# Converting float64 gate weights beside the expert items alone, in two buffers, with one multiplication handed to ScalarE and GpSimd

## The chip, the cores and the metric

The kernel runs on one core of a Trainium2 chip. The core has a matrix engine (TensorE, PE in the profile, with its weight loads shown apart as PEld), a vector engine (VectorE, DVE), ScalarE (ACT), GpSimd (POOL) and SyncE (SP), which issues the transfers. They run side by side and wait for each other by semaphores. Each engine takes its instructions strictly in the order of its own queue. The metric is the device time of one execution in microseconds (us), as the median of several runs.

## The reference, cut to what matters

```python
def _moe_ref(x, domain_probs, w1, w2):          # x: 1536 tokens x 512, out of a windowed attention
    p = domain_probs / (domain_probs.sum(-1, keepdims=True) + 1e-09)
    out = np.zeros((N, D), dtype=np.float32)
    for e in range(E):                           # 4 experts, d_ff 1024
        h = np.maximum(x @ w1[e], 0.0)
        out += p[:, e:e + 1] * (h @ w2[e])
    return out

def _moe2_ref(x, w_a, w_b, w_out):               # d_ff 1536
    a = x @ w_a
    b = x @ w_b
    return a * b @ w_out

attn_out = _attn_ref(q, k, v, n_sink, window)    # 2 batches, 8 heads, 768 positions, 64 wide
x = attn_out.transpose(0, 2, 1, 3).reshape(B * S, H * D)
x = _moe_ref(x, ...)
return _moe2_ref(x, moe2_w_a, moe2_w_b, moe2_w_out)
```

The three weights of the last, gated layer (`w_a`, `w_b`, `w_out`) arrive as float64. [...]

## The kernel before

**Precision.** All products are made from float32 numbers cut into a high and a low part (`split`: the high part is a rounded copy, the low part the difference). A product is then three matmuls: high by high, high by low, low by high (`three`).

**Stages.** The program is recorded in three pieces, and each is put in order and issued by `nc.run()`. The first has the attention of batch 0 and the first two pieces of the experts for batch 0. The second has the attention of batch 1 beside most of the experts' pieces for batch 0. The third, in the trace from about 375 us on, has no attention. It has the last expert piece of batch 0, then 16 *items* of experts for batch 1 (about 395 to 645 us; below the expert items), then 12 items of the gated layer for batch 0 (from about 645 us on), then 12 for batch 1 (to the end).

**One item.** `seven` makes the up products of an item by a Strassen-like scheme of seven products in two banks of PSUM, `m` and `n`. Between them intermediate results have to leave the banks: copies `r1`, `r5`, `u2` (in the trace `r` and `u`, by ScalarE or VectorE) and sums `c0` to `c2` (`c`, by VectorE). Only then may TensorE write the bank again. Six output tiles of the item before are laid between these products (`dh`, `dl`, `hh`, `hl` in the trace).

**Weights of an item.** `ups` loads `rawu` (one buffer), forms four sums of its quarters (`sums`) and splits seven blocks into `uh` and `ul` (two buffers each). For batch 1 of the experts and of the gated layer the split blocks come back from memory (`store`, `keeping`), so the 16 expert items of batch 1 have no splitting to do, and the 12 gated items of batch 0 have all of it. While the gated items of batch 0 run, the expert results of batch 1 are also transposed into tokens (`turned`: three transposes of `y` into a bank, a copy `x` out of it, then sums and splits).

**Converting the gate weights** (`gate_weights`). There are 36 parts of 128x512 numbers: for each of 12 blocks one of `w_a`, one of `w_b`, one of `w_out`. A part is loaded into one of two buffers `raw64` (in the trace `raw`; low words `l`, high words `h`, interleaved). Two halves `t` and `u` of a buffer `tu`, of which there is one, take the steps: ScalarE squares the high word (`tf`), VectorE makes five instructions on them, and a last addition goes to VectorE or GpSimd. Then the part is written to memory (`gu` or `gd`), from where `ups` and `downs` load it as `rawu` and `rawd`. How fast the parts are recorded beside the items is set by `PARTS` and `PARTS_LATE`: 1.6 parts an item to the end of the expert items, then 1.2.

**What sets the order.** `Plan.run` is a list scheduler. Each instruction has a cost and a due time; at each step the engine that can begin first takes its most urgent ready instruction. An instruction with two ways (`either`, used by `copied` for ScalarE or VectorE, and by `combined` for GpSimd or VectorE) goes to whichever takes it first. `shares` marks the instructions that the planner takes to need a port that VectorE and GpSimd have in common: every GpSimd instruction but a memset, and VectorE's with SBUF operands alone, either two of them or a copy or scalar operation. `begin` puts off such a one until the other engine's has ended. Nothing of these times reaches the chip: only the order and the choice of engine do, with the waits that the data need.

Of the kernel before, what the change touches and what calls it, by code (L numbers as in the profile page):

```python
# [9 lines left out]
F32 = mybir.dt.float32  # L10
F32R = mybir.dt.float32r
BF16 = mybir.dt.bfloat16
I32 = mybir.dt.int32
U32 = mybir.dt.uint32
ACTF = mybir.ActivationFunctionType
ALU = mybir.AluOpType
# [3 lines left out]
P = 128  # L20
# [75 lines left out]
class Plan:  # L96
# [163 lines left out]
    def run(self, ahead=8, idle=None):  # L260
# [15 lines left out]
        ready = {e: [] for e in "TVSGD"}  # L276
# [31 lines left out]
        for _ in nodes:  # L308
            best = None
            for e, some in ready.items():  # L310
                if e == "T":
                    some = [x for x in some if rank[x["n"]] < first + ahead]
                if not some:
                    continue
                now = max(free[e], min(x["ready"] for x in some))
                if e not in "TD":
                    while True:
                        can = [x for x in some if x["ready"] <= now and fits(x, e, now)]
                        if can:
                            break  # L320
                        later_ = [x["ready"] for x in some if x["ready"] > now]
                        if not later_:
                            break
                        now = min(later_)
                    if not can:
                        continue
                    x = min(can, key=urgent)

                    soon = [
                        y for y in some if now < y["ready"] < now + x["ways"][e][0]  # L330
                        and y["due"] < min(x["due"] - self.MORE, at + self.NEAR) and fits(y, e, y["ready"])
                    ]
                    if soon:
                        y = min(soon, key=urgent)
                        short = [z for z in can if now + z["ways"][e][0] <= y["ready"]]
                        x = min(short, key=urgent) if short else y
                        now = max(now, x["ready"])

                    start = begin(x, e, now)
                    if start > now:  # L340
                        short = [
                            z for z in can if begin(z, e, now) == now and now + z["ways"][e][0] < start + self.NEAR_PORT
                        ]
                        x, start = (min(short, key=urgent), now) if short else (x, start)
                    now = start
                else:
                    x = min((x for x in some if x["ready"] <= now), key=urgent)
                if best is None or now < best[0]:
                    best = now, x, e
            now, x, e = best  # L350
            for f in x["ways"]:
                ready[f].remove(x)
            x["e"], (cost, x["calls"], shared) = e, x["ways"][e]
            x["cost"] = cost
            if e == "T" and idle:
                if any(self.region(args[0] if args else kw["out"])[0] == idle[0].tensor.name for _, args, kw in x["calls"]):
                    idle = None
                elif not free[e]:
                    x["idle"] = self.IDLE_FIRST, idle
                elif now - free[e] > self.IDLE:  # L360
                    x["idle"] = int((now - free[e] - self.IDLE_LEFT) / self.IDLE_COST), idle
            free[e] = now + cost
            if shared:
                port[e] = now + cost
            order.append(x)
            if e == "T":
                at = max(at, x["at"])
                done.add(rank[x["n"]])
                while first in done:
                    first += 1  # L370
            for u in users[x["n"]]:
                y = nodes[u]
                y["ready"] = max(y["ready"], now + cost + lag(x, y))
                left[u] -= 1
                if not left[u]:
                    release(y)
# [12 lines left out]
def tile_kernel(ctx, tc, a0, a1, vs, limit, dp, w1, w2, wa, wb, wo, out):  # L389
# [11 lines left out]
    NV = E * FP  # L401
# [906 lines left out]


    CONVERT_STEPS = 11  # L1310
    PARTS, PARTS_LATE = 1.6, 1.2

    def gate_weights(room):

# [18 lines left out]
        for n, (_, dst) in enumerate(parts):  # L1333
            raw, ahead = ahead, fetch(n + 1) if n + 1 < len(parts) else None
            for _ in range(3):
                yield
            tu = room("tu")
            l, h, t, u = raw[:, :, 0], raw[:, :, 1], tu[:, 0:512], tu[:, 512:1024]
            tf, uf = t.bitcast(F32), u.bitcast(F32)
            nc.scalar.activation(out=tf, in_=h.bitcast(F32), func=ACTF.Square)  # L1340
            nc.vector.tensor_scalar(
                out=u, in0=h, scalar1=3, scalar2=0x3FFFFFFF, op0=ALU.logical_shift_left, op1=ALU.bitwise_and
            )
            yield
            nc.vector.scalar_tensor_tensor(
                out=u, in0=h, scalar=-0x40000000, in1=u, op0=ALU.bitwise_and, op1=ALU.bitwise_or
            )
            yield
            nc.vector.scalar_tensor_tensor(
                out=uf, in0=tf, scalar=W_LOW * W_LOW, in1=uf, op0=ALU.is_ge, op1=ALU.mult  # L1350
            )
            yield
            nc.vector.tensor_scalar(out=t, in0=u, scalar1=-0x800000, scalar2=None, op0=ALU.bitwise_and)
            yield
            nc.vector.scalar_tensor_tensor(
                out=tf, in0=l.bitcast(U32), scalar=2.0 ** -52, in1=tf, op0=ALU.mult, op1=ALU.mult
            )
            yield
            combined(uf, uf, tf, add)
            yield  # L1360
            yield
            nc.sync.dma_start(out=dst, in_=form(uf, dst))
            yield

    def convert_steps(parts):

        return CONVERT_STEPS * parts
# [94 lines left out]
    with ExitStack() as st:  # L1462
# [103 lines left out]
        with ExitStack() as s2:  # L1566
# [10 lines left out]

            plains[-1].bank, plains[-1].apart = bank, True
            plain = Expert(items[own - 1], x, wu, wd, y0, bank)
            room = lambda name: p.g.tile([P, 1024], I32, tag=name, name=name, bufs={"raw64": 2, "tu": 1}[name])  # L1580
            w = Stream(gate_weights(room))
            for n, _ in enumerate(run([plain], bank, plains[-1], freed)):
                u.to(UP_STEPS * (own + (n + 1) / ITEM_STEPS))
                d.to(DOWN_STEPS * (own - 1 + (n + 1) / ITEM_STEPS))
                w.to(convert_steps(PARTS * (n + 1) / ITEM_STEPS))
            flagged = Stream(need_general(bank))
            open_ = {}
            run_ = [Expert(it, x, wu, wd, y1, bank, True, open_) for it in items[own:own + NV]]
# [13 lines left out]
            for n, _ in enumerate(run(run_, bank, plain, freed)):  # L1602
# [10 lines left out]
                for b, i in enumerate((3, NV + 2)):  # L1613
                    k = n - start(i) - 10
                    if k > 0:
                        tr[b].to(k / ITEM_STEPS)
                at, turn = 1 + (n + 1) / ITEM_STEPS, NV + 1
                w.to(convert_steps(PARTS * min(at, turn) + PARTS_LATE * max(at - turn, 0)))
            d.finish()
            rest_of(run_[-1])  # L1620
            nc.run()
# [62 lines left out]
```

## Time and profile before

| | |
|---|---|
| median of 3 runs | 938.14 us (936.51 to 940.12) |
| the profiled execution | 936.52 us, of which its span, first to last instruction, 934.6 us |
| busy in the span | TensorE 907.0 us (97%), weight loads 818.0 us (88%), VectorE 743.2 us (80%), ScalarE 399.1 us (43%), GpSimd 321.1 us (34%) |
| chain of work that ended last | TensorE 72%, VectorE 17%, DMA 6%, issue 2%, ScalarE 2%, GpSimd 1% |
| granted TensorE clock, mean | 0.997 |

A busy time is the union of the engine's instructions. Matmuls overlap in it: one that shows 0.40 us lets the next begin after about 0.23 us, so a wait of TensorE is longer than the idle time shown before the matmul that ends it.

### The profile page before, as it was taken

To read this page: it belongs to the slowest core of one execution; us is meant where nothing else is said; L and a number is where in the kernel's file an instruction comes from. 1 tells how busy PE (TensorE), PEld (TensorE's weight loads), DVE (VectorE), ACT (ScalarE), POOL (GpSimd) and SP (SyncE) were. 2 spreads that over 40 slices of the span, in tenths; PEclk is the share of its full clock that TensorE was granted. 3 is DMA by queue.
4 is the path that set the end of the run, shared out by engine and by line. 5 is a ranking of instruction groups with operands and counts; after the bars stand their busy time and mean duration, and the time that the engine had idled before them with its cause. 6 is when DMAs were issued, how large, how long until landed. Compare 5 with 4: busy or idle time off the path is not lost.

```text
span 934.6 us, 14309 instructions
## 1 busy us (share of the span) xinstructions
PE 907.0 (97%) x5051; PEld 818.0 (88%) x5051; DVE 743.2 (80%) x1511; ACT 399.1 (43%) x933; POOL 321.1 (34%) x326
## 2 busy tenths in 40 slices
PE   9999989999999999999999999999898999999996
PEld 7888889888889899889899898989797889999995
DVE  8999789999999998986877878798888985333333
ACT  6886367766667655321222211243444453111111
POOL 5484556474545635210200200035254543100100
PEclk9999999999999999999999999999999999999999
DMA  5350468885666665778686877777779778755552
GB/s 170 112 193 1 153 222 297 278 278 185 238 223 246 221 225 181 237 273 306 220 297 234 297 239 274 263 251 256 256 246 320 276 280 316 250 205 202 205 197 94
DMA packets 84609, 215.35 MB, mean 230 GB/s; under 512 B 7856, under 2 KB 42032, under 8 KB 84528
## 3 DMA queue, kind: packets, MB, share of 16 engines
q1 hardware_dynamic: 84528, 214.35, 65.8%
q8 instruction: 41, 0.67, 0.3%
q14 instruction: 40, 0.33, 0.1%
HBM read 130.97 MB, written 83.36 MB: 229 GB/s over the span
## 4 chain that ended last, share of the span: by engine, by line
PE 72%; DVE 17%; DMA 6%; issue 2%; ACT 2%; POOL 1%; SPq 0%; DVEq 0%; ACTq 0%; POOLq 0%
PE bank L383 71%; DVE tu L383 2%; DMA rawu<-gu 2%; DVE y L383 2%; DVE ul L383 1%; DVE kk L383 1%; DVE pp L383 1%; DVE c L383 1%; PE bank L381 1%; DVE hl L383 1%; DVE pt L383 1%; DVE sums L383 1%; DVE x L383 1%; DMA araw<-in_a 1%; DMA rawu<-in_w 1%
## 5 line engine op out<-in xcount | busy, mean ns | idle before, releaser
L383 PE MATMUL bank<-dh,hh 128*128 128x512 f32 x528 | 209.6, 397 | 0.2 <-DVE y L383 0.2
L383 PE MATMUL bank<-dl,hh 128*128 128x512 f32 x528 | 208.5, 395 | 0.0
L383 PE MATMUL bank<-dh,hl 128*128 128x512 f32 x528 | 208.0, 394 | 0.0
L383 PE MATMUL bank<-xh,uh 128*128 128x384 f32 (+1 forms) x384 | 128.5, 335 | 2.4 <-DVE r L383 1.7
L383 PE MATMUL bank<-xl,uh 128*128 128x384 f32 (+1 forms) x384 | 127.0, 331 | 0.1
L383 PE MATMUL bank<-xh,ul 128*128 128x384 f32 (+1 forms) x384 | 126.5, 330 | 0.0
L383 PEld LDWEIGHTS bank<-dl,hh 128*128 128x128 f32 x528 | 99.0, 187 | 21.7
L383 PE MATMUL bank<-th,uh 128*128 128x384 f32 x324 | 109.4, 338 | 3.5 <-DVE c L383 1.9
L383 PEld LDWEIGHTS bank<-dh,hh 128*128 128x128 f32 x528 | 99.2, 188 | 13.7 <-DVE y L383 0.6
L383 PEld LDWEIGHTS bank<-dh,hl 128*128 128x128 f32 x528 | 99.2, 188 | 12.6
L383 PE MATMUL bank<-tl,uh 128*128 128x384 f32 x324 | 109.5, 338 | 0.2
L383 PE MATMUL bank<-th,ul 128*128 128x384 f32 x324 | 109.1, 337 | 0.0
L383 ACT ACTIVATE r<-bank 128x384 f32<-128x384 f32 x74 | 36.3, 490 | 146.8 <-PE bank L383 146.6
L383 ACT ACTIVATE hh<-c 128x384 fp32r<-128x384 f32 (+1 forms) x99 | 51.3, 519 | 93.7 <-DVE c L383 92.6
L383 DVE TENSOR_TENSOR c<-bank,r 128x384 f32<-128x384 f32 x108 | 59.8, 553 | 34.2 <-PE bank L383 33.7
L383 DVE SCALAR_TENSOR_TENSOR y<-bank,prob,y 128x512 f32<-128x512 f32 x108 | 79.8, 743 | 6.1 <-PE bank L383 5.2
L383 DVE TENSOR_TENSOR c<-bank,u 128x384 f32<-128x384 f32 x54 | 29.9, 553 | 66.8 <-PE bank L383 63.8
L383 PEld LDWEIGHTS bank<-xh,uh 128*128 128x128 f32 x384 | 72.4, 189 | 8.2 <-DVE r L383 2.3
L383 PEld LDWEIGHTS bank<-xl,uh 128*128 128x128 f32 x384 | 72.3, 188 | 4.7 <-DVE xl L383 0.3
L383 POOL TENSOR_TENSOR ul<-sums,uh 128x256 fp32r<-128x256 f32 (+1 forms) x44 | 44.1, 1009 | 82.8 <-DMA ul<-ue 53.2
L383 PEld LDWEIGHTS bank<-xh,ul 128*128 128x128 f32 x384 | 72.3, 188 | 0.0
L383 PEld LDWEIGHTS bank<-th,uh 128*128 128x128 f32 x324 | 61.1, 189 | 7.8 <-DVE c L383 3.1
(152 smaller groups left out, 1830.1 us busy)
## 6 DMA issues: line engine op xcount, KB each, us to landing
ue<-uh SPq DMA_DIRECT2D x14, 896.0 KB, 4.3
ue<-ul SPq DMA_DIRECT2D x14, 896.0 KB, 5.8
uh<-ue SPq DMA_DIRECT2D x14, 896.0 KB, 4.7
ul<-ue SPq DMA_DIRECT2D x14, 896.0 KB, 6.7
ug<-uh SPq DMA_DIRECT2D x12, 896.0 KB, 5.3
ug<-ul SPq DMA_DIRECT2D x12, 896.0 KB, 7.6
uh<-ug SPq DMA_DIRECT2D x12, 896.0 KB, 4.5
ul<-ug SPq DMA_DIRECT2D x12, 896.0 KB, 6.3
```

The source lines that it names most:

```text
L381: self.nc.tensor.matmul(out=bank, lhsT=lhs, rhs=rhs, start=True, stop=True)
L383: call(*args, **kw)
```

## The change

Five things change. (1) `PARTS` is 2.3 and `PARTS_LATE` is gone; conversion no longer begins beside the last expert piece of batch 0 (the line `w.to` in that loop is removed) but with the expert items of batch 1, so that its 36 parts fill about 15.7 items. (2) `tu` has two buffers. (3) The one VectorE instruction that multiplied the low word by a power of two and by `tf` becomes two: ScalarE scales the low words, in place in `raw`, and a multiplication by `combined` may go to GpSimd or VectorE. (4) One of the two empty steps of a part goes, the new step takes its place. (5) In the planner, an instruction that needs the shared port, and could begin while the other engine is free, looks whether that engine has a ready, more urgent instruction for the port that only it can do. If so its own start is put off by that one's cost, in the planner's reckoning.

```diff
@@ class Plan, run
                         x, start = (min(short, key=urgent), now) if short else (x, start)
+                    if x["ways"][e][2] and free[other[e]] <= start:
+
+                        rivals = [
+                            y for y in ready[other[e]] if e not in y["ways"] and y["ways"][other[e]][2]
+                            and y["ready"] <= start and y["due"] < x["due"]
+                        ]
+                        if rivals:
+                            start += min(rivals, key=urgent)["ways"][other[e]][0]
                     now = start
@@
-    PARTS, PARTS_LATE = 1.6, 1.2
+    PARTS = 2.3
@@ def gate_weights(room)
             nc.vector.tensor_scalar(out=t, in0=u, scalar1=-0x800000, scalar2=None, op0=ALU.bitwise_and)
             yield
-            nc.vector.scalar_tensor_tensor(
-                out=tf, in0=l.bitcast(U32), scalar=2.0 ** -52, in1=tf, op0=ALU.mult, op1=ALU.mult
-            )
+            lf = l.bitcast(F32)
+            nc.scalar.activation(out=lf, in_=l.bitcast(U32), func=copy, scale=2.0 ** -52)
+            yield
+            combined(tf, tf, lf, ALU.mult)
             yield
             combined(uf, uf, tf, add)
-            yield
             yield
             nc.sync.dma_start(out=dst, in_=form(uf, dst))
@@
-            room = lambda name: p.g.tile([P, 1024], I32, tag=name, name=name, bufs={"raw64": 2, "tu": 1}[name])
+            room = lambda name: p.g.tile([P, 1024], I32, tag=name, name=name, bufs={"raw64": 2, "tu": 2}[name])
             w = Stream(gate_weights(room))
             for n, _ in enumerate(run([plain], bank, plains[-1], freed)):
                 u.to(UP_STEPS * (own + (n + 1) / ITEM_STEPS))
                 d.to(DOWN_STEPS * (own - 1 + (n + 1) / ITEM_STEPS))
-                w.to(convert_steps(PARTS * (n + 1) / ITEM_STEPS))
@@
-                at, turn = 1 + (n + 1) / ITEM_STEPS, NV + 1
-                w.to(convert_steps(PARTS * min(at, turn) + PARTS_LATE * max(at - turn, 0)))
+                w.to(convert_steps(PARTS * (n + 1) / ITEM_STEPS))
```

What this makes of the order is shown at three places. All three are in the third piece; the order of the second piece is the same before and after on every engine, and in the first piece TensorE, VectorE, ScalarE and GpSimd run the tail of batch 0's attention (from 53 to 95 us of the trace) in another order.

The first place is VectorE in the middle of the expert items, from the start of a part on. `tu` and `raw` belong to the conversion, `c`, `r`, `u` and `hl` to the item. Before:

```order
L383 TENSOR_SCALAR tu_4014<-raw_0_4012 128x512
L383 SCALAR_TENSOR_TENSOR tu_4014<-raw_0_4012,tu_4014 128x512
L383 COPY u_0_1601<-bank_99 128x384
L383 SCALAR_TENSOR_TENSOR tu_4014<-tu_4014 128x512
L383 TENSOR_TENSOR c_0_1607<-bank_101,u_0_1601 128x384
L383 TENSOR_SCALAR tu_4014<-tu_4014 128x512
L383 SCALAR_TENSOR_TENSOR tu_4014<-raw_0_4012,tu_4014 128x512
L383 SCALAR_TENSOR_TENSOR hl_193<-c_0_1607,hh_192 128x384
L383 TENSOR_TENSOR tu_4014<-tu_4014 128x512
```

After, at a like place of the expert items:

```order
L391 TENSOR_SCALAR tu_4019<-raw_1_4017 128x512
L391 TENSOR_TENSOR c_0_1607<-bank_99,u_0_1601 128x384
L391 SCALAR_TENSOR_TENSOR tu_4019<-raw_1_4017,tu_4019 128x512
L391 SCALAR_TENSOR_TENSOR tu_4019<-tu_4019 128x512
L391 TENSOR_TENSOR c_0_1608<-bank_101,r_0_1600 128x384
L391 SCALAR_TENSOR_TENSOR hl_176<-c_0_1607,hh_175 128x384
L391 TENSOR_SCALAR tu_4019<-tu_4019 128x512
L391 SCALAR_TENSOR_TENSOR hl_184<-c_0_1608,hh_183 128x384
L391 TENSOR_TENSOR tu_4019<-tu_4019,raw_1_4017 128x512
```

The second instruction that read `raw` with `tu` is gone; where VectorE has the multiplication it reads `tu` and `raw` as the last row does. Counted over all 36 parts, VectorE has the multiplication 17 times and the addition 18 times (before: the addition 29 times), GpSimd 19 and 18 times (before: the addition 7 times), and ScalarE has 36 instructions `raw<-raw` more.

The second place is VectorE where the first gated item of batch 0 begins and the last results `y` of the experts leave their banks. Before:

```order
L383 SCALAR_TENSOR_TENSOR y_0_4005<-bank_100,prob,y_0_4005 128x512
L383 SCALAR_TENSOR_TENSOR tu_4014<-raw_1_4013,tu_4014 128x512
L383 SCALAR_TENSOR_TENSOR y_0_4006<-bank_102,prob,y_0_4006 128x512
L383 SCALAR_TENSOR_TENSOR tu_4014<-tu_4014 128x512
L383 TENSOR_SCALAR tu_4014<-tu_4014 128x512
L383 SCALAR_TENSOR_TENSOR tu_4014<-raw_1_4013,tu_4014 128x512
L383 TENSOR_TENSOR c_0_1607<-bank_101,u_0_1601 128x384
```

After:

```order
L391 SCALAR_TENSOR_TENSOR y_0_4005<-bank_100,prob,y_0_4005 128x512
L391 SCALAR_TENSOR_TENSOR y_0_4006<-bank_102,prob,y_0_4006 128x512
L391 TENSOR_TENSOR sums_196<-rawu_163 128x256
L391 TENSOR_TENSOR c_0_1607<-bank_101,u_0_1601 128x384
L391 TENSOR_TENSOR sums_196<-sums_196,rawu_163 128x256
L391 CAST uh_171<-sums_196 128x512
L391 TENSOR_TENSOR c_0_1608<-bank_99,r_0_1600 128x384
```

No instruction on `tu` stands on VectorE from here on; before, 52 of them still came in the gated items.

The third place is TensorE at the fifth triple of transposes (`ident,y`, of `turned`) in the gated items of batch 0. Before:

```order
L383 MATMUL bank_102<-dl_182,hh_194 128x512
L383 MATMUL bank_99<-ident,y_0_4007 128x128
L383 MATMUL bank_99<-ident,y_0_4008 128x128
L383 MATMUL bank_99<-ident,y_0_4009 128x128
L383 MATMUL bank_99<-yt_0_4017,uh_171 128x384
L383 MATMUL bank_99<-yt_0_4018,uh_171 128x384
```

After:

```order
L391 MATMUL bank_99<-ident,y_0_4009 128x128
L391 MATMUL bank_100<-dh_181,hh_194 128x512
L391 MATMUL bank_100<-dh_181,hl_195 128x512
L391 MATMUL bank_100<-dl_182,hh_194 128x512
L391 MATMUL bank_102<-dh_181,hh_194 128x512
L391 MATMUL bank_102<-dh_181,hl_195 128x512
L391 MATMUL bank_102<-dl_182,hh_194 128x512
L391 MATMUL bank_99<-yt_0_4014,uh_171 128x384
```

Before, the product that writes the transposes' bank again followed at once; after, six output matmuls on other banks stand between. The fourth triple moves in the same way.

## Rows read from the trace of the kernel before

**Rows 1.** Stretches: length, busy us of PE, PEld, DVE, ACT, POOL, PEclk, DMA share, GB/s
```profile
50.00:100.00 50.00, 48.36 (x356) 42.09 (x355) 44.53 (x124) 31.47 (x87) 28.75 (x33) 1.00 0.20 71
...
125.00:375.00 250.00, 245.44 (x1353) 222.64 (x1352) 237.29 (x496) 160.57 (x386) 134.33 (x136) 1.00 0.69 241
395.00:645.00 250.00, 250.00 (x1262) 225.08 (x1261) 202.52 (x362) 61.52 (x116) 39.55 (x32) 1.00 0.76 264
...
645.00:775.00 130.00, 122.25 (x628) 109.02 (x627) 114.25 (x186) 59.34 (x127) 56.45 (x48) 1.00 0.80 276
775.00:925.00 150.00, 150.00 (x779) 139.27 (x778) 58.46 (x118) 25.26 (x53) 16.26 (x14) 1.00 0.58 213
```

**Rows 2.** TensorE's waits from 645 to 775 us: for whom, total, times, longest
```profile
PE bank L383 <- ACT r L383: 3.5, 3, 2.0
PE bank L383 <- DVE c L383: 1.6, 3, 0.9
PE bank L383 <- DVE ul L383: 1.4, 1, 1.4
PE bank L383 <- ACT x L383: 1.2, 2, 0.6
```

**Rows 3.** TensorE around 669 us: start, duration, instruction, idle before it
```profile
668.72 0.40 PE L383 MATMUL bank<-dh,hl 128*128 128x512 f32 x1
668.95 0.40 PE L383 MATMUL bank<-dl,hh 128*128 128x512 f32 x1
670.24 0.44 PE L383 MATMUL bank<-th,uh 128*128 128x384 f32 x1 [0.90 <-ACT r L383]
670.52 0.33 PE L383 MATMUL bank<-tl,uh 128*128 128x384 f32 x1
670.69 0.34 PE L383 MATMUL bank<-th,ul 128*128 128x384 f32 x1
```

**Rows 4.** ScalarE around 673 us, columns as in rows 3
```profile
672.51 0.63 ACT L383 ACTIVATE uh<-sums 128x512 fp32r<-128x512 f32 x1 [2.32 <-DVE sums L383]
673.04 0.47 ACT L383 ACTIVATE r<-bank 128x384 f32<-128x384 f32 x1
```

**Rows 5.** VectorE around 740 us
```profile
740.29 1.48 DVE L383 SCALAR_TENSOR_TENSOR tu<-tu 128x512 f32<-128x512 f32 x1
```

**Rows 6.** GpSimd around 740 us
```profile
740.05 1.18 POOL L383 TENSOR_TENSOR x<-x 128x384 f32<-128x384 f32 x1
```

**Rows 7.** Instructions on `tu`: ns min/median/max, first and last start us
```profile
L383 DVE SCALAR_TENSOR_TENSOR tu<-raw,tu x72: 673/691/1879, 376.9 to 742.5; 128x512 int32<-128x512 int32 x36, 128x512 f32<-128x512 uint32 x36
L383 ACT ACTIVATE tu<-raw x36: 657/672/689, 364.5 to 732.0; 128x512 f32<-128x512 f32 x36
L383 DVE TENSOR_SCALAR tu<-raw x36: 409/423/1131, 376.2 to 736.3; 128x512 int32<-128x512 int32 x36
L383 DVE SCALAR_TENSOR_TENSOR tu<-tu x36: 678/684/1483, 378.4 to 740.3; 128x512 f32<-128x512 f32 x36
...
L383 DVE TENSOR_TENSOR tu<-tu x29: 676/691/1503, 382.1 to 743.6; 128x512 f32<-128x512 f32 x29
...
L383 POOL TENSOR_TENSOR tu<-tu x7: 1289/1301/1302, 427.7 to 604.1; 128x512 f32<-128x512 f32 x7
```

**Rows 8.** Busy time on `tu` by stretch: VectorE, ScalarE, GpSimd
```profile
395.00:645.00 250.00, 90.70 (x145) 16.78 (x25) 9.08 (x7) 1.00 0.76 264
645.00:775.00 130.00, 40.94 (x52) 5.36 (x8) 0.00 (x0) 1.00 0.80 276
```

**Rows 9.** TensorE around the fifth triple of transposes
```profile
720.82 0.49 PE L383 MATMUL bank<-ident,y 128*128 128x128 f32 x3
721.89 0.62 PE L383 MATMUL bank<-yt,uh 128*128 128x384 f32 x2 [0.58 <-ACT x L383]
```

**Rows 10.** TensorE at its last wait of the gated items
```profile
759.26 0.55 PE L383 MATMUL bank<-ident,y 128*128 128x128 f32 x3 [0.30 <-DVE c L383]
```

**Rows 11.** TensorE's waits from 125 to 375 us, columns as in rows 2
```profile
PE bank L383 <- DVE r L383: 0.9, 1, 0.9
```

## Prediction, made before the changed kernel was run

> **What bounds the kernel now.** I read the busy times by stretch first, because an engine at 97% over the whole span says nothing of where the rest lies. They show three kinds of stretch [rows 1]. Beside the expert items (395 to 645 us) TensorE has no idle time at all, though VectorE is busy for 202.52 of 250 us. In the gated items of batch 1 (775 to 925) it has none either. In the gated items of batch 0 (645 to 775) it is busy for 122.25 of 130 us, so 7.75 us are missing, and there VectorE is busy for 114.25 us, 88%. In the second piece with attention (125 to 375) 4.56 us are missing. TensorE's own work does not change, so the change can only give what TensorE waits, above all in the gated items of batch 0, and can only take by new waits.
>
> The list of TensorE's waits in that stretch [rows 2] accounts for it: 3 waits for `r`, 3 for `c`, 1 for `ul`, 2 for `x`, together 7.7 us. None of these is a conversion. But the engines run in order, and the conversion stands ahead of what TensorE needs: 40.94 us of VectorE's time in this stretch are `tu` [rows 8], more than a third of its work. The longest wait shows how it reaches TensorE. `r`, a copy out of a bank, came on ScalarE at 673.04 behind `uh<-sums`, which had waited 2.32 us for VectorE's sums [rows 4]. VectorE was late with the sums, as it had conversion steps among them.
>
> The idle figures are too small. At 669 us the matmul that waited started 1.29 us after the one before it, where 0.23 us is the usual step, so 1.06 us were lost where 0.90 is shown; and the next matmul then came 0.28 us later where 0.17 is usual [rows 3]. With 0.16 and 0.11 us for each of nine waits, 7.75 becomes 10.2 us.
>
> **What the change removes there.** In the gated items every `tu` step goes, 52 on VectorE and 8 on ScalarE, 40.94 and 5.36 us [rows 8], and with them the conversion's loads and writes from SyncE's queue, in which the load of `rawu` stands behind them. What is left of VectorE's work is 114.25 - 40.94 = 73.3 us in some 120 us, 61%. TensorE's order also changes at the fourth and fifth triple of transposes. At the fifth the next product waited 1.07 us from the start of the transposes, 0.58 of it idle for the copy `x` [rows 9]; six matmuls at 0.23 us now stand between and cover the copy. That is one of the two `x` waits, the other goes alike.
>
> How much of the 10.2 us goes I read from the end of the same stretch. The last conversion step is at 743.6 [rows 7]; from there to 775 us there is one wait, 0.30 us idle, 0.57 with the additions above [rows 10], in 31 us of the same splitting and turning. Were the whole 130 us like that, 2.4 us would stay. So the gated items give 10.2 - 2.4 = **7.8 us**. The bounds are 10.2, if nothing is left, and 3.8, if only the two waits for `x` (1.2 + 0.5 us) and a quarter of the other 8.5 go.
>
> **What it adds beside the experts.** A part costs VectorE now 0.423 twice, 0.691 twice, 0.684 and the addition, 0.691 in 29 of 36 cases: 3.47 us [rows 7], the second scalar form taken like the first. After, it is 0.423 twice, 0.691, 0.684, the multiplication at 0.691 in 17 of 36 and the addition in 18 of 36: 2.89 us. By the order all but the last two or so of the 36 now fall in the 250 us; for all, it is 104 us for the 90.70 that stand there [rows 8]. VectorE comes to 202.5 - 90.7 + 104 = 216 us, 86%. ScalarE's new scaling is priced by its squaring, 0.672 us; 36 of them make 24 us, and with the 11 squarings that move in, 7.4 us, ScalarE goes from 61.5 to 93 of 250 us, so this costs nothing while ScalarE idles more than half of the time; were it full, a `r` behind each would cost 0.67. The second `tu` takes away waits for the write of a part; these were on no path of TensorE here.
>
> GpSimd gets 30 instructions more of 1.30 us [rows 7], 39 us on 39.55 busy. They cost by what they do to VectorE. At 740 us a step of VectorE that usually takes 0.684 took 1.48 us while GpSimd's sum of two SBUF operands ran beside it from 740.05 to 741.23 [rows 5 to 7]. So one costs VectorE between 0 and 1.3 us. I take 0.4, half of the 0.8 seen, since a VectorE instruction that reads a bank is put beside GpSimd's by the planner where there is one. That is 12 us: VectorE at 228 of 250 us, 91%.
>
> What 91% costs TensorE is bounded by the stage that has it already: from 125 to 375 us VectorE is busy for 237.29 us, 95%, and GpSimd for 134 us, and TensorE misses 4.56 us [rows 1]. Of these only 0.9 us are a wait that an expert item has too, for `r` [rows 11]; the rest belongs mostly to attention. I take **0.9 us** lost, between 0 and 4.6.
>
> **The first piece.** The planner's new rule puts the tail of batch 0's attention in another order on four engines. The trace shows none of this, so I bound it: TensorE misses 1.64 us from 50 to 100 us, and VectorE is busy for 44.53 of 50 us [rows 1]. A gain is at most 1.6. VectorE takes over three casts of 128x512 and some smaller ones from ScalarE and gives others away, in sum about one such instruction more; for a loss I take the bound of 2.5 us, the idle of the stage with attention scaled to its length and more than doubled. I take **0.5 us** lost. The second piece is in the same order and should take the same time.
>
> **Sum.** -7.8 + 0.9 + 0.5 = -6.4 us. The profiled execution took 936.5 us, so its like would take 930.1; the median of the runs shown is 1.6 us above it, and 938.1 - 6.4 = **931.7 us**.
>
> **Rivals.**
> *The loads set the gated items, not VectorE.* ScalarE's and VectorE's queues there also wait for `rawu`, which is in one buffer, and the wait for `r` may come from that. Against it: after 743.6 us the same loads go on and the waits all but end. By the lower bound above it gives 3.8 us: 938.1 - 3.8 + 1.4 = 935.7 us.
> *GpSimd locks VectorE out beside the experts, slower than before.* If each of the 30 instructions costs VectorE its whole 1.30 us, VectorE needs 216 + 39 = 255 us in 250. The point from which it decides is (250 - 216) / 30 = 1.13 us for each. Then TensorE has at least the waits of the stage at 95% and the 5 us that do not fit, 9.6 us instead of 0.9; the parts run over into the gated items and keep half of their waits, so that these give 3.9: 938.1 + 9.6 + 0.5 - 3.9 = 944.3 us. For it speaks the stretched row; against it that the stage at 95% has 134 us of GpSimd beside 237 of VectorE, and runs almost without waits for `r` and `c`. The Trainium skill (SBUF — State Buffer, "SBUF: two separate sides") states the rule of this rival: VectorE with two SBUF inputs and GpSimd share a pair of ports as an exclusive lock for a whole instruction, and the later one blocks entirely. The stretched row agrees with it; by the rule alone, with every instruction meeting its worst case, the time would be the one just given.
> *The attention's tail gets slower* by the bound of 2.5 us or somewhat more: 938.1 - 7.8 + 0.9 + 3.5 = 934.7 us.
> *More than forecast*: the experts lose nothing and the first piece gains its 1.6: 938.1 - 7.8 - 1.6 = 928.7 us.
>
> **Chances.** The forecast, 929.5 to 933.8 us, has 0.58. Loads 0.18, lock 0.10, tail 0.08, more 0.06. A change of 0.5%, 4.7 us, is about what a measurement of this kernel can tell from none: faster is below 933.4, slower above 942.8. The forecast (0.54 of its 0.58) and "more" give 0.60 faster; loads, tail, and what is left of the forecast and a mild lock give 0.33; the lock in full 0.07 slower. The range of 8 in 10 leaves out the lock and the end of the loads' case: 928.5 to 937.0.
>
> **What would show it.** From 645 to 775 us no `tu` on any engine but a last write, VectorE near 73 us of that work, and TensorE's idle time near 2 us instead of 7.75, with no wait for `x`. From 395 to 645 TensorE busy for at least 249 of 250 us, VectorE 220 to 235, GpSimd about 78, ScalarE about 93. In the first 100 us TensorE's idle time within 1 us of before. Wrong would be: waits of TensorE for `r`, `c` or `hh` among the expert items that add to over 4 us, or gated items that still wait for `r` behind `uh`, with SyncE issuing `rawu` no earlier than now.

## The result and the profile after

The changed kernel takes **924.52 us** (median of 4 runs, 923.63 to 924.78), the kernel before, timed beside it, 937.33 (936.39 to 940.12). The ratio is 0.9857, with a 95% interval of 0.9833 to 0.988: 12.8 us faster, twice the 6.4 us forecast, and below the range of 928.5 to 937.0. The profiled execution took 924.3 us with a span of 922.5.

The stretches of the changed kernel, to be read against [rows 1] (columns as there):

```profile
50.00:100.00 50.00, 48.24 (x364) 42.77 (x363) 45.33 (x128) 29.24 (x84) 29.19 (x35) 1.00 0.20 71
125.00:375.00 250.00, 245.66 (x1351) 222.17 (x1351) 237.43 (x493) 161.42 (x386) 131.91 (x134) 1.00 0.71 244
395.00:645.00 250.00, 250.00 (x1261) 224.96 (x1260) 214.07 (x383) 89.29 (x167) 73.91 (x56) 1.00 0.86 294
645.00:775.00 130.00, 129.78 (x683) 119.80 (x682) 91.10 (x166) 53.80 (x114) 36.40 (x35) 1.00 0.72 260
```

In the gated items of batch 0 TensorE's idle time fell from 7.75 to 0.22 us, and it got 683 matmuls into the 130 us instead of 628. Beside the experts it still has no idle time, with VectorE at 214.07 us. The waits of TensorE there, where [rows 2] had nine of four kinds:

```profile
PE bank L391 <- DVE c L391: 0.2, 1, 0.2
```

The instructions on `tu` of the changed kernel, to be read against [rows 7]:

```profile
L391 DVE TENSOR_SCALAR tu<-raw x36: 410/427/1300, 383.6 to 620.4; 128x512 int32<-128x512 int32 x36
L391 POOL TENSOR_TENSOR tu<-tu,raw x19: 1297/1323/1633, 390.3 to 585.3; 128x512 f32<-128x512 f32 x19
L391 DVE TENSOR_TENSOR tu<-tu x18: 677/679/692, 391.8 to 627.4; 128x512 f32<-128x512 f32 x18
```

The last step is at 627.4 us, where it was at 743.6. The parts now follow each other by some 6.8 us (383.6 to 627.4 over 36), where one took 10.2 (376.2 to 743.6). The triple of transposes of [rows 10] starts at 747.08 us without a wait:

```profile
747.08 0.49 PE L391 MATMUL bank<-ident,y 128*128 128x128 f32 x3
```

The first triple of the gated items stands at 664.68 us before and at 663.60 after, so 11.1 of the 12.1 us by which the span got shorter lie between these two places, and 1.1 ahead of them.

### The profile page after: what moved, and what is told of

It reads as the page before. It is cut to its first block, busy times and chain, and to the rows that moved or that the text cites. A ratio compares the mean times of both kernels' runs of the same rounds, so it can differ in the third digit from the quotient of the medians.

```text
span 922.5 us, 14376 instructions
## 1 busy us (share of the span) xinstructions
PE 902.0 (98%) x5051; PEld 817.2 (89%) x5051; DVE 727.9 (79%) x1506; ACT 415.6 (45%) x962; POOL 330.9 (36%) x338
## 4 chain that ended last, share of the span: by engine, by line
PE 82%; DVE 14%; issue 1%; ACT 1%; POOL 0%; POOLq 0%; DVEq 0%
PE bank L391 81%; DVE y L391 2%; DVE kk L391 1%; DVE pp L391 1%; DVE hl L391 1%; DVE c L391 1%; DVE pt L391 1%; PE bank L389 1%; DVE st L391 1%; DVE x L391 1%; DVE tl L391 1%; DVE xl L391 1%; DVE ul L391 1%; DVE r L391 0%; DVE sums L391 0%
## 5 line engine op out<-in xcount | busy, mean ns | idle before, releaser
L391 ACT ACTIVATE hh<-c 128x384 fp32r<-128x384 f32 (+1 forms) x103 | 53.5, 519 | 71.8 <-DVE c L391 71.4
L391 PEld LDWEIGHTS bank<-tl,uh 128*128 128x128 f32 x324 | 60.8, 188 | 3.2 <-DVE tl L391 0.6
```

The costliest lines, as they stand in the source:

```text
L391: call(*args, **kw)
```

## The experiments

The forecast said that the gated items wait because conversion steps stand among them, and that the faster pace takes the steps out. Each expectation names the theories that were held against each other when it was written. Ratios are to the kernel before, timed beside each, with 95% intervals.

**One part of the change at a time, from the kernel before.** The pace alone:

```
-    PARTS, PARTS_LATE = 1.6, 1.2
+    PARTS = 2.3
...
-                w.to(convert_steps(PARTS * (n + 1) / ITEM_STEPS))
...
-                at, turn = 1 + (n + 1) / ITEM_STEPS, NV + 1
-                w.to(convert_steps(PARTS * min(at, turn) + PARTS_LATE * max(at - turn, 0)))
+                w.to(convert_steps(PARTS * (n + 1) / ITEM_STEPS))
```

> The kernel before with the pace alone changed: 2.3 parts an expert item, none beside the last piece of batch 0; one tu, the multiplication on VectorE, the planner as before. Theory A (the place of the steps is all): TensorE's idle time from 645 to 775 us falls from 7.75 to under 1 us, and the time to 925 to 929 us; VectorE beside the expert items comes to some 235 of 250 us (202.5 - 90.7 + 36 x 3.47), which costs TensorE at most 1 to 2 us. Theory B (the lighter parts are needed): VectorE is then too full beside the expert items, TensorE waits there for r and c by 4 us or more, and the time is 931 to 936 us.

Measured: 946.16 us, ratio 1.0103 (1.0082 to 1.0123), slower, and above what either theory gave. The pace did not take the steps out: 41 VectorE steps are left in 645 to 775, the last at 719.8 us, and TensorE still idles 4.4 us there. With one buffer a part still took 9.9 us, where the pace asks for 6.8 (2.3 parts in an item of 15.6 us). In its place something new was lost at the start of the third piece (the column of busy times as in rows 1):

```profile
355.00:395.00 40.00, 32.57 (x147) 27.39 (x146) 36.66 (x48) 17.63 (x33) 26.15 (x20) 0.87 0.51 171
```

TensorE is busy for 32.57 of 40 us at a mean clock of 0.87. The planner's new rule alone (the eight lines of the diff in the function that lines up):

> The kernel before with the planner's new rule alone. Theory A: the first piece has the new order and gains 0 to 1 us, and 1.7 us more if the half clock at 123 us is gone with it; in the gated items the waits stay at 6 to 8 us of idle time. So 934.5 to 938 us. Theory C: 930 us or less, with the idle time of 645 to 775 us halved.

Measured: 933.99 us, ratio 0.9971 (0.9956 to 0.9987). The rule gives some 0.3% by itself; 6.0 us of idle stay in 645 to 775.

The second buffer alone, one digit of the kernel before:

```
-            room = lambda name: p.g.tile([P, 1024], I32, tag=name, name=name, bufs={"raw64": 2, "tu": 1}[name])
+            room = lambda name: p.g.tile([P, 1024], I32, tag=name, name=name, bufs={"raw64": 2, "tu": 2}[name])
```

> The kernel before with a second buffer tu alone; pace, multiplication and planner as before. Theory E: the gated items keep their 9 parts, so their waits stay at 5 us of idle time or more: 934 to 938 us. Theory D (the second buffer carries the gain by itself): 930 us or less.

Measured: 925.62 us, ratio 0.9889 (0.9871 to 0.9907). That is 10 us of the 12.8: the two medians are 1.1 us apart, and by the ratios, each to its own timing of the kernel before, some 3 us are left for the rest of the change. Its stretch of gated items:

```profile
645.00:775.00 130.00, 129.99 (x682) 119.68 (x682) 100.87 (x191) 52.29 (x112) 37.48 (x34) 1.00 0.76 275
```

TensorE idles 0.01 us there, although 18 VectorE steps on `tu` (11.27 us) still stand in the stretch. The last step of all is an addition on GpSimd at 684.7 us.

**One part of the change undone, from the changed kernel.** One buffer `tu` in place of two:

> The changed kernel with one buffer tu. Theory A: a part waits for the write of the one before, as it did, on VectorE's queue by 1 to 2 us at a time, but beside the expert items TensorE has room for it: 924.5 to 926.5 us, no wait of TensorE over 1 us in all from 395 to 645 us. Theory D (the second buffer carries the faster pace): the parts fall behind, into the gated items, VectorE waits for the writes there, and the time is 928 us or more.

Measured: 946.14 us, ratio 1.0118 (1.0088 to 1.0148). With one buffer the rest of the change is a loss, and most of it lies at the start of the third piece, where neither theory placed it: from 340 to 395 us TensorE is busy for 45.78 us, 54.92 in the kernel before. VectorE's order at the start of the third piece shows how (start, duration, instruction, idle before it):

```profile
373.88 1.59 DVE L391 TENSOR_SCALAR tu<-raw 128x512 int32<-128x512 int32 x1 [0.36 <-DMA gu<-tu]
375.51 1.09 DVE L391 SCALAR_TENSOR_TENSOR tu<-raw,tu 128x512 int32<-128x512 int32 x1
376.72 1.56 DVE L391 SCALAR_TENSOR_TENSOR tu<-tu 128x512 f32<-128x512 f32 x1
378.31 0.83 DVE L391 TENSOR_SCALAR tu<-tu 128x512 int32<-128x512 int32 x1
379.24 0.69 DVE L391 TENSOR_TENSOR tu<-tu,raw 128x512 f32<-128x512 f32 x1
379.97 0.69 DVE L391 TENSOR_TENSOR tu<-tu 128x512 f32<-128x512 f32 x1
380.58 0.55 DVE L391 SCALAR_TENSOR_TENSOR hl<-bank,hh 128x384 fp32r<-128x384 f32 x1
```

and TensorE's the wait that follows from it:

```profile
381.28 0.66 PE L391 MATMUL bank<-th,uh 128*128 128x384 f32 x1 [7.62 <-DVE hl L391]
```

A whole part, six steps, stands ahead of `hl`; its first step had waited for the write of the part before to land. The next part shows the chain in numbers: first step at 389.67, write issued at 393.62 and landed at 397.47, the next part's first step at 397.56.

The other parts undone: the planner's rule out; the pace and start of before; the low words multiplied on VectorE again; and, against the rival of the ports, all 72 multiplications and additions put on GpSimd:

```
-            combined(tf, tf, lf, ALU.mult)
+            nc.gpsimd.tensor_tensor(out=tf, in0=tf, in1=lf, op=ALU.mult)
...
-            combined(uf, uf, tf, add)
+            nc.gpsimd.tensor_tensor(out=uf, in0=uf, in1=tf, op=add)
```

> The changed kernel without the planner's new rule for the shared port. Theory A: the gated items of batch 0 keep under 1 us of waits, as the rule isn't what empties them; the first piece goes back to its old order, so the time is 924.5 us plus what the rule gives there: 0 to 1 us from its order, and 1.7 us more if the 3.4 us at half of the granted clock at 123 us belong to the old order. So 924.5 to 927.5 us. Theory C (the rule gives much of the gain, by keeping GpSimd from holding VectorE up): 929 us or more, with waits for r and c among the expert or gated items.

> The changed kernel with the pace of before, 1.6 parts an item and then 1.2, begun beside the last piece of batch 0; two tu, the lighter parts and the rule stay. Theory E: some 9 parts still stand in the gated items, each with 2.9 us of VectorE for 3.5; TensorE's idle time from 645 to 775 us is 4 to 7 us and the time 930 to 935 us. Rival (the lighter parts empty the gated items by themselves): under 2 us of idle time there, 927 us or less.

> The changed kernel with the old multiplication, one instruction on VectorE that scales and multiplies, and ScalarE's scaling left out; two tu, pace 2.3 and the planner's rule stay. Theory E (with two buffers the pace is what counts, the lighter parts are not needed): no run of tu steps ahead of hl at the start of the third piece, VectorE at 225 to 238 us of 250 beside the expert items, TensorE's waits there under 1.5 us, the time 924 to 927 us. Theory B (VectorE is too full without the lighter parts): waits for r, c or hl of 3 us or more beside the expert items, the time 929 us or more.

> The changed kernel with the multiplication and the addition of all 36 parts forced to GpSimd: 72 of its instructions at 1.30 us, 94 us, instead of 37. VectorE gives up 35 instructions, 24 us. If each GpSimd instruction costs VectorE its whole length, VectorE's busy time from 395 to 645 us rises to some 214 - 24 + 35 x 1.3 = 236 us; at 0.4 us each it falls to 204 us. Theory A: in both cases TensorE waits under 1.5 us more, 924 to 927 us. The lock rival: 930 us or more, with waits for c or hl behind stretched VectorE instructions.

Measured: without the rule 925.67 us (0.9895, 0.9874 to 0.9915), with the old pace 924.12 (0.9875, 0.9857 to 0.9892), with the multiplication on VectorE 928.26 (0.991, 0.989 to 0.993), with all 72 on GpSimd 924.02 (0.9874, 0.9856 to 0.9892). So neither rule nor pace carries the gain, and the scaling on ScalarE is worth some 4 us at most, beside two buffers: the 928.26 lie between what its two theories gave, and TensorE is busy there for all of the 250 us beside the experts, so VectorE is not too full without it. The rival of the ports falls. Of the kernel with 72 instructions on GpSimd:

```profile
395.00:645.00 250.00, 250.00 (x1261) 225.02 (x1260) 211.55 (x327) 95.89 (x180) 121.55 (x88) 1.00 0.83 286
```

GpSimd is busy for 121.55 us, VectorE for 211.55, and TensorE has no idle time.

**Which half of the second buffer.** A part's write to memory reads `u`; `t` only passes values inside the part. The kernel before with `t` in one buffer and `u` in two, the kernel before with a third buffer for the loads instead (`"raw64": 3`), and the changed kernel with one buffer and the old pace:

```
-            tu = room("tu")
-            l, h, t, u = raw[:, :, 0], raw[:, :, 1], tu[:, 0:512], tu[:, 512:1024]
+            t, u = room("tt"), room("tu")
+            l, h = raw[:, :, 0], raw[:, :, 1]
...
-            room = lambda name: p.g.tile([P, 1024], I32, tag=name, name=name, bufs={"raw64": 2, "tu": 1}[name])
+            room = lambda name: p.g.tile([P, 1024 if name == "raw64" else 512], I32, tag=name, name=name, bufs={"raw64": 2, "tt": 1, "tu": 2}[name])
```

> The kernel before, with the two halves of tu as tiles of their own: t in one buffer, u, which the part's write to memory reads, in two. Pace, multiply and lining-up rule are those of before. What tells the theories apart is which half of the second buffer matters. Theory 'the wait for the write is the chain': with two buffers of u a part's first steps no longer wait for the landing of the part before it (3.6 to 3.8 us, and an interval of 10.2 us a part in the kernel before), so the parts run ahead as with two whole buffers: 924 to 928 us, idle of TensorE in 645 to 775 under 2 us, last convert step before 700 us. Rival 'two whole parts have to be under way, since t passes from VectorE to the other engines inside a part': one t still holds the parts one behind another, 931 us or more, idle in 645 to 775 of 4 us or more, last step after 720 us.

> The kernel before with three buffers of raw64, into which the weights are loaded, in place of two, and one buffer tu as before. Theory 'tu is the chain': the loads were never what the next part waited for, so nothing moves: 934 to 940 us, TensorE idle 4 to 8 us in 645 to 775, last step near 740 us. Rival 'any buffer more lets parts run ahead, since the load of a part is released late': 930 us or less, last step before 710 us.

> The changed kernel with one buffer tu in place of two and with the pace and the start of the kernel before; the low words are still scaled on ScalarE and the lining-up rule stays. Theory 'the buffer sets where the steps stand': the parts again end one after the other, with steps in the gated items to about 740 us; TensorE waits there 4 to 7 us between 645 and 775, and no bunch of convert steps stands ahead of hl between 360 and 395, since the pace asks for no more than the buffer gives: 931 to 937 us. Rival 'lighter parts and the rule empty the gated items by themselves': last step before 700 us, idle in 645 to 775 under 2 us, 924 to 927 us.

Measured: two `u` and one `t` 925.20 us (0.988, 0.9863 to 0.9896), three load buffers 937.17 (0.9997, 0.9978 to 1.0016), one buffer with light parts, rule and old pace 931.62 (0.9952, 0.9935 to 0.9968). Nearly the whole gain comes with the buffer that the write reads. The third kernel still has 51 VectorE steps in 645 to 775 and 5.8 us of idle, so lighter parts and the rule don't empty the gated items. Against the changed kernel with one buffer it differs by the pace alone: with one buffer the faster pace costs 1.7% (0.9952 against 1.0118).

**Place or rank.** The forecast held the steps' place among the gated items to be the harm. So the kernel with two buffers alone got its last nine parts tied to their place in the program:

```
             c = p.c.tile([P, HT], F32, tag=name, name=name)
             nc.vector.tensor_tensor(out=c, in0=a, in1=b, op=add)
+            mark["c"] = c
...
+            if n >= 27:
+                nc.vector.tensor_copy(raw[:, 0:1].bitcast(F32), mark["c"][:, 0:1])
```

> The kernel before with two buffers tu, and with the last nine of the 36 parts tied to their place in the program by a copy of one column of the current item's c into the buffer of the load, ahead of the load: those parts can't run ahead of the gated items any more. Nine copies of one column are added. The theory of the forecast, 'convert steps between the gated items' links are what they wait for': TensorE's idle in 645 to 775 is 4 to 8 us as before, 930 to 937 us. Rival 'the wait for the write of a single buffer, which makes steps urgent all at once, is what they wait for, and steps there harm nothing when two parts can be under way': under 2 us idle in 645 to 775 although VectorE still runs 25 or more convert steps there, 924 to 929 us.

Measured: 925.80 us (0.9888, 0.9871 to 0.9904). The stretch of gated items, all engines:

```profile
645.00:775.00 130.00, 129.30 (x683) 119.68 (x682) 113.21 (x211) 57.10 (x120) 40.39 (x37) 1.00 0.84 297
```

and of it the busy time on `tu` (VectorE, ScalarE, GpSimd, as in [rows 8]):

```profile
645.00:775.00 130.00, 25.77 (x41) 4.68 (x7) 1.29 (x1) 1.00 0.84 297
```

VectorE is as busy as before (113.21 against 114.25 us) and runs 41 steps there where it ran 52, and TensorE idles 0.7 us instead of 7.75. With two buffers the place is not the harm.

What was left is the rank: the planner puts a step ahead of the links once it is late against its due time, 15 us behind its place in the program. Two kernels have two buffers and every step, load and write of a part ranked 30 us early, the second with the nine parts held back as well; one has a single buffer and no due time by place (`part` marks what belongs to a part):

```
+        for x in nodes:
+            x["due"] -= 30000.0 if x["part"] is not None else 0.0
...
-            due = x["at"] if x["e"] == "T" else min(x["at"] + self.SLACK, self.at - x["cost"])
+            due = x["at"] if x["e"] == "T" else min(x["at"] + self.SLACK if x["part"] is None else self.at, self.at - x["cost"])
```

> The kernel before with two buffers tu, and every convert step ranked 30 us earlier than its place gives. Theory 'rank': the steps go ahead of hl and c at the start of the third piece as with one buffer at the faster pace, TensorE waits 3 to 8 us between 340 and 400 or loses as much in 395 to 645, 930 to 946 us. Theory 'one part in flight': with two buffers rank does nothing, 923 to 928 us, idle of 340 to 645 under 2 us.

> As the kernel with every convert step ranked 30 us early and two buffers, and with the last nine parts held back among the gated items by copies of one column of c, as in the run held back without that rank (925.80 us, idle of 0.7 us in 645 to 775). Theory 'rank': the links of the gated items wait again, TensorE idles 4 us or more in 645 to 775. Theory 'one part in flight': under 2 us there. What the start of the third piece loses is read apart, from 340 to 400, and is that of the run without holding back.

> The kernel before with one buffer tu, where the planner gives the convert steps no due time of their own (15 us behind their place in the program before); only the loads that read the converted weights still press them. The order shows fewer steps in the experts and more in the gated items than before. Theory 'rank': links wait since late steps are put ahead of them; without that TensorE idles under 3 us in 645 to 775 although more than 55 convert steps stand there, 926 to 931 us. Theory 'one part in flight': steps among the links cost whatever their rank; idle there is 6 to 12 us, 934 to 942 us.

Measured: pressed 947.68 us (1.0109, 1.0086 to 1.0132), pressed and held back 957.62 (1.022, 1.0201 to 1.0239). The first is a little above the 946 us that the theory of the rank gave at most. The rank brings the loss back with two buffers. From 340 to 395 us TensorE of the first of them has 43.00 us of work, where the kernel before has 54.92; in the second the gated items wait too, 7.4 us in 645 to 775, and VectorE shows the order of the single buffer again:

```profile
718.89 0.68 DVE L387 SCALAR_TENSOR_TENSOR tu<-raw,tu 128x512 int32<-128x512 int32 x1
719.68 1.04 DVE L387 SCALAR_TENSOR_TENSOR tu<-tu 128x512 f32<-128x512 f32 x1
720.75 1.10 DVE L387 TENSOR_SCALAR tu<-tu 128x512 int32<-128x512 int32 x1
721.89 1.63 DVE L387 SCALAR_TENSOR_TENSOR tu<-raw,tu 128x512 f32<-128x512 uint32 x1
723.56 1.09 DVE L387 TENSOR_TENSOR tu<-tu 128x512 f32<-128x512 f32 x1
724.58 1.07 DVE L387 TENSOR_TENSOR hl<-c,hh 128x384 fp32r<-128x384 f32 x1
```

with this on TensorE:

```profile
725.70 0.79 PE L387 MATMUL bank<-dh,hl 128*128 128x512 f32 x1 [5.11 <-DVE hl L387]
```

The single buffer without a due time by place took 970.55 us (1.0364, 1.034 to 1.0388), above what either theory gave. Its parts go on from 393.3 to 803.8 us, 11.4 each. The planner explains this: the steps take only what the links leave free, and the gated items' loads of the converted weights, which carry due times of their own, then press the late ones. No trace shows due times, so this is argued. The busy time on `tu` by stretch:

```profile
395.00:645.00 250.00, 72.30 (x115) 13.34 (x20) 8.24 (x6) 1.00 0.71 248
645.00:775.00 130.00, 65.15 (x71) 8.03 (x12) 0.00 (x0) 0.96 0.76 264
775.00:850.00 75.00, 16.59 (x24) 2.00 (x3) 0.00 (x0) 0.91 0.70 252
```

So a single buffer can't finish in time by free places alone. This run doesn't tell the two theories apart: if the planner's account holds, the consumers give the steps back the rank that was taken away.

## Why the prediction was wrong

**The step that failed** is the one that costed the second buffer at nothing: "The second `tu` takes away waits for the write of a part; these were on no path of TensorE here." No wait of TensorE names the write, but the chain of work that ended last goes through it, in the kernel before already (start, duration, what):

```profile
674.31 4.71 DMA gd<-tu
679.02 0.02 issue
679.04 0.95 DVE tu L383
679.99 0.48 DVE c L383
680.47 0.04 issue
680.51 8.60 PE bank L383 x45
```

VectorE's row for that step shows what happened: the first step of a part stood on the queue ahead of the sum `c` that TensorE needed, and waited until the write of the part before had landed.

```profile
679.04 0.95 DVE L383 TENSOR_SCALAR tu<-raw 128x512 int32<-128x512 int32 x1 [0.98 <-DMA gd<-tu]
```

A second write of a part, 4.91 us from 731.33, is on the same chain. VectorE itself stood idle for such landings for only 1.3 us from 645 to 775; that the larger part of the harm is parts that come late is argued from this and from the runs with two buffers. With one buffer the 36 parts are one chain (in the changed kernel with one buffer a first step had to wait out the 3.85 us from 393.62 to 397.47 until the landing), which took 9.9 us a part at the pace of 2.3, of which VectorE's work is 3.5. The buffer moved the last step further than the pace did: it was at 743.6 us, at 719.8 with the faster pace and one buffer, at 684.7 with the old pace and two. I credited the pace with what the buffer does. The change holds both, so this step got the cause wrong; the number went wrong by the terms below, above all by the gated items at 7.8 us, which gave 11.1.

**The mechanism in the gated items** was half right. The waits do come from conversion steps ahead of the links on VectorE's queue, as [rows 4] read, but not from them alone: before the longest wait VectorE had first stood idle for the load of `rawu`, and then run a conversion step.

```profile
668.13 0.43 DVE L383 TENSOR_TENSOR sums<-rawu 128x256 f32<-128x256 f32 x1 [2.35 <-DMA rawu<-gu]
668.47 1.23 DVE L383 SCALAR_TENSOR_TENSOR tu<-tu 128x512 f32<-128x512 f32 x1
```

That the steps' place in that stretch is the harm fell with the kernel held back: 41 steps cost 0.7 us there. What costs, with two buffers, is steps that are ranked ahead of the links, shown by the two pressed kernels. That late steps' rank is also what put them ahead in the kernel before follows from the planner's rule and these runs, but wasn't shown on that kernel by itself; the run that took the rank away made the chain end too late.

**The terms.** The gated items gave 11.1 us between the two triples, not 7.8. The 10.2 us that I held to be all there was were too few, and the 2.4 that I left standing too many. VectorE has 91.10 us of work there and not the 73 forecast, and TensorE does not wait for it. Beside the experts I took 0.9 us of loss and there is none: VectorE is at 214.07 us and not 228, since the 30 added instructions on GpSimd did not stretch it: without `tu`, it has 111.5 us of work there (214.07 less 102.60) where it had 111.8 (202.52 less 90.70). ScalarE (89.29, forecast 93) and GpSimd (73.91, forecast 78) came out near. For the first piece I took 0.5 us of loss, and with what follows up to the gated items it is 1.1 of gain. By the starts of the same matmuls in both traces the changed kernel is 1.0 us ahead at 115 us, after the tail in its new order, 2.5 at 129, after a stretch at half the clock that the kernel before had, and 1.6 at 419, after the start of the third piece. That stretch comes and goes from one execution to the next (below), so 1.5 us of what lies between these two executions are luck. With 11.1 and 1.1 for 7.8 less 1.4, the forecast would have been about right.

**The rivals.** "The loads set the gated items" was not tried as it stands: the third buffer, which changed nothing, went to the loads of the conversion, and the rival speaks of `rawu`. The traces speak against it. From 645 to 775 us ScalarE and VectorE waited for `rawu` for 25.7 and 4.9 us in the kernel before, and for 1.5 and 2.2 us in the kernel held back, although a load took as long there (5.4 us in the median from issue to landing, 5.0 before) and more was moved (297 GB/s against 276). In the kernel before eight of the nine loads were issued within 0.4 us of the last instruction that read the buffer, so SyncE's queue did not hold them back, and they came late because those instructions did. What a second `rawu` would give is open. "GpSimd locks VectorE out" fell: 72 instructions there cost TensorE nothing. A stretch of some 0.4 us for each is there: in that kernel the 138 steps left to VectorE from 395 to 645 us take 104.93 us, 0.76 each, where the medians of the four forms in [rows 7] make 0.555, which is 28 us for 70 instructions on `tu` on GpSimd. VectorE had room for them, as it was rid of 72. By the rule of the Trainium skill (SBUF — State Buffer, "SBUF: two separate sides") each could cost up to its whole time, 1.43 us here; the trace has a row that agrees (the step of 1.63 us at 721.89 above, 0.69 in the median, ran beside a two-input instruction of GpSimd from 721.53 to 722.97), but the 0.4 us say that far from every instruction meets one. The case "more than forecast" had the right direction and 0.06.

**What would have shown it ahead.** [rows 7] has the numbers: 36 parts over 376.2 to 743.6 us are 10.2 us each, for 3.47 us of VectorE's work, while VectorE idled for 47 of the 250 us beside the experts [rows 1]. I read the durations there and not the interval. The interval alone would not have done, though: 1.6 parts in an item of 15.6 us ask for 9.8 us each, and between 395 and 645 us the 26 first steps stand 9.77 us apart (397.7 to 642.0). The pace of the kernel before was about as slow as the chain, and only the faster pace with one buffer, or the chain of work above, tells the two apart.

## What to carry to other kernels

Divide the time over which a background stream runs by its pieces, and compare it with the work of one and with the interval that its pace asks for: where it is far above the work, look for the buffer that makes one piece wait for the last, the one that a write to memory reads above all, before touching the pace. In a planner with due times, a stream that can't keep its pace isn't background any more: it goes ahead of the work it was to stay behind, and asking for a faster pace makes that worse. A second buffer of half the size that was added (`u` alone) gave nearly the whole gain here (925.20 us, 924.52 for the whole change).

## What the runs showed of the hardware

**A wait costs more than itself.** After waits of some us TensorE was granted its lower clock for a while, in the cases below. In the kernel with two buffers and steps ranked early, around the start of the third piece:

```profile
340.00:370.00 30.00, 29.63 (x161) 26.89 (x160) 25.97 (x48) 16.03 (x34) 11.97 (x14) 1.00 0.53 183
370.00:378.00 8.00, 5.63 (x27) 4.56 (x25) 8.00 (x12) 4.22 (x8) 8.00 (x6) 1.00 0.82 299
378.00:398.00 20.00, 10.73 (x27) 7.96 (x28) 18.12 (x19) 3.55 (x7) 13.48 (x10) 0.55 0.37 121
```

The granted clock is 0.55 over the 20 us from 378 (1.0 is 2.4 GHz, and 0.5 the other level, 1.2 GHz), and a 128x384 matmul in a row of such shows 0.52 us where it shows 0.33 elsewhere. Around the fall of the clock TensorE had waited 3.41 us for `th` and 1.76 for `tl`. Of these 20 us it was idle for 9.3, and in most of the other 10.7 it worked at half speed. With one buffer and the faster pace, the six steps ahead of `hl` (7.62 us of wait) and what followed made a kernel slower by some 10 us, although its gated items idled for only 2.0 us in 645 to 775.

The kernel before has such a stretch near 122 us, after the first piece, in the profiled execution (length, busy us, PEclk, DMA as in rows 1):

```profile
122.00:127.00 5.00, 5.00 (x24) 5.00 (x23) 3.88 (x11) 3.15 (x11) 1.42 (x2) 0.66 0.41 136
```

The changed kernel has none there:

```profile
122.00:127.00 5.00, 5.00 (x32) 5.00 (x31) 4.89 (x13) 3.08 (x11) 1.89 (x2) 1.00 0.61 176
```

That is 24 matmuls at a clock of 0.66 against 32 at 1.00. No edit decides it. The kernels with two buffers alone, with two `u` and one `t`, and held back run that stretch in the order of the kernel before; the first has a clock of 1.00 from 122 to 127 us, the other two 0.66 and 0.71. So it comes and goes between executions of one order, and it is worth under 2 us.
